# Moving casts, transfers and check steps in a hand-interleaved attention and FFN kernel

## The chip, the cores and the metric

The kernel runs on one core of one Trainium2 chip. The metric is device time in microseconds (us) of one execution of the whole program; lower is better. Its engines work side by side, each on its own list of instructions in order: TensorE (PE, matrix products), ScalarE (ACT), VectorE (DVE), GpSimd (POOL) and SyncE (SP, which here issues transfers). Instructions wait for each other through semaphores. Transfers (DMA) are issued by SP, ACT and POOL and run on 16 DMA engines.

## The reference

Causal attention with a decay bias, followed by a gated FFN:

```python
# q, k, v: (8 batches, 8 heads, 576, 64); s: (8, 8, 576)
scores = (q @ k^T) / sqrt(64)
cum    = cumsum(max(s, 0))
scores = where(causal, -1e9, scores + min(-(cum[i] - cum[j]), 0))
attn   = softmax(scores);  x = attn @ v          # as (4608 tokens, 512)
xn     = x / sqrt(mean(x^2) + 1e-6) * rms_g
g, val = xn @ w_gate, xn @ w_val                  # (512 -> 1536)
out    = (g * sigmoid(g) * val) @ w_out           # (1536 -> 512)
```

All inputs and outputs are float32; the products run in bf16.

## The kernel before, in words

The output's 4608 tokens are cut into 9 chunks of 512. `ffn(c)` computes one chunk: for each of 12 blocks `fb` of the hidden width, TensorE makes a gate product `Gp` (L668, four matmuls) and a value product `Vp` (L677), ScalarE a tanh `T` (L671), VectorE `U` = (T + 1) Gp (L680) and `Ht` = U Vp (L673); then four output blocks of 12 matmuls each (L690), copied out by ScalarE (`osb`, L695) and stored by a transfer on SP (L697). The products write `psF` buffers in PSUM, of which there are four in rotation: `Gp` is released by `U`, `Vp` by `Ht`.

Between these products the kernel calls `step()`, 36 times in a chunk. `slot` counts the calls, `phase()` the calls since the chunk began. Each call emits pieces of the attention of later batches, so TensorE's list is FFN products with attention pieces between them. The order is fixed when the program is built: lags are counted in steps, not in time. One call does, in this order:

- `x_scale` of the next block of x (L338, VectorE: x times its 1/rms `al_all` times `rms_g`), three steps after the second half of its attention output; then `xt_dma` (L348), a transpose on SP into `xnT`, which the FFN reads
- one item of `act_side` (ScalarE's casts, and issues of K and Q loads)
- if no block of x was moved: a transposing transfer of K or Q, `kq_dma` (L171, SP), from the list `x_seq`, at most every second step
- one item of `v_side` (issues of V loads, L175, on GpSimd's queue), in odd steps
- one item of `pool_side` (GpSimd's casts of K and Q to bf16, L141 and L149, or issues of loads of K, L155) and one of `dve_side` (VectorE's casts and magnitude checks, L369 and L375)
- a score step `S` (L250 matmuls, exps on ScalarE L274, causal mask on GpSimd L283), or else a transpose of x on TensorE, an attention output step `AV` (L300, L306, VectorE's L313 and L315, a sum of squares on ScalarE L321 or VectorE L325, 1/rms on GpSimd L328 and L331), and a transpose of K or Q on TensorE (`t_step`, L184)

A block is 128 rows of a batch's 576 (five blocks, the last of 64). For batches 0 and 1 K and Q are transposed on TensorE and copied by ScalarE (L192) or VectorE (L190); later ones use the transposing transfers. In batch 1 the cast of row group r of K or Q is one instruction of 128x512; "K2" below means K with r = 2. Before its first FFN chunk the kernel computes batch 0's attention without the stepper; the list of what follows, for batch 1, stands at L887 to L899. `need(c)` sees to it that the blocks of x that chunk c reads have been emitted.

`verdict()` (L741) reduces collected maxima to one flag, which says whether the fast path was exact enough; a general path follows it behind a branch. It needs VectorE reductions, a transpose of `stat` on TensorE (L750), another reduction, a second transpose (L754), an exp on ScalarE and five small VectorE instructions. It is emitted as one piece after chunk 7 (the eighth), before chunk 8, the last.

Of the kernel before, what the change touches and what calls it, by code (L numbers as in the profile page):

```python
# [12 lines left out]
AF = mybir.ActivationFunctionType  # L13
ALU = mybir.AluOpType
AX = mybir.AxisListType
# [4 lines left out]
DROP_MAX = 576.0 * 2.0 ** -24  # L20
RANGE_MAX = 75.0
# [5 lines left out]
def kernel(  # L27
# [91 lines left out]
    def psT32():  # L119
        return pp.tile([128, 512], FP32, name="psT32", tag="T", bufs=1)  # L120
# [14 lines left out]
    def cast(eng, b, w, r0, r1, h0=0, h1=H):  # L135
        o = kqn[:, b % 2, w, r0:r1, h0:h1, :]
        i = kq32[:, w].rearrange("p h (r d) -> p r h d", d=D)[:, r0:r1, h0:h1, :]
        if eng is nc.scalar:
            eng.activation(out=o, in_=i, func=AF.Copy)
        else:  # L140
            eng.tensor_copy(out=o, in_=i)  # L141
# [258 lines left out]
    def ready(lag, *key):  # L400
        return at(*key) + lag <= slot[0]
# [27 lines left out]
    def phase():  # L429

        return slot[0] - first[0]
# [167 lines left out]
    def step(bare=False):  # L599
# [13 lines left out]
                    done["XT", b, qb] = slot[0] + 4  # L613
                    moved = True
        run_side(act_side)
        if not moved and x_seq and slot[0] - last["X"] >= 2:
            b, w, c = x_seq[0]
            if (ready(2, "cast", b, 1) and ready(1, "S", b - 2, 4, 0)
                    and (w == 1 or ready(7, "K", b, c))):
                x_seq.pop(0)  # L620
                kq_dma(b, w, c)
                done["X", b, w, c] = last["X"] = slot[0]
                if b >= KB and (w, c) == (0, NSC - 1) and b + 2 < B:
                    casts(b + 2)
        bare = bare or chunk[0] == 0 and 30 <= phase() <= 33
        if slot[0] % 2 and not bare:
            run_side(v_side)
        if not bare:
            run_side(pool_side)
# [109 lines left out]
            lambda i=i: row(i) for i in range(3)] + [over])  # L739

    def verdict():  # L741
        nc.vector.tensor_reduce(out=stat[:, 0:1], in_=acc, axis=AX.X, op=ALU.max)
        okc = mp.tile([128, B * NSC], FP32, name="okc")
        nc.vector.tensor_scalar(out=okc, in0=ss_all, scalar1=SS_MAX, scalar2=None, op0=ALU.is_le)
        low = mp.tile([128, 1], FP32, name="low")
        nc.vector.tensor_reduce(out=low, in_=okc, axis=AX.X, op=ALU.min)
        nc.vector.tensor_scalar(out=stat[:, 3:4], in0=low, scalar1=-1.0, scalar2=1.0,
                                op0=ALU.mult, op1=ALU.add)
        ps = psT32()
        nc.tensor.matmul(ps[0:4, 0:128], lhsT=stat, rhs=ident_f, is_transpose=True)  # L750
        mx = mp.tile([4, 1], FP32, name="mx")
        nc.vector.tensor_reduce(out=mx, in_=ps[0:4, 0:128], axis=AX.X, op=ALU.max)
        ps2 = psT32()
        nc.tensor.matmul(ps2[0:1, 0:4], lhsT=mx, rhs=ident_f[0:4, 0:4], is_transpose=True)  # L754
        g = mp.tile([1, 8], FP32, name="g")
        nc.vector.tensor_copy(out=g[:, 0:4], in_=ps2[0:1, 0:4])

        nc.vector.tensor_scalar(out=g[:, 4:5], in0=g[:, 0:1], scalar1=g[:, 0:1], scalar2=8.0625,
                                op0=ALU.mult, op1=ALU.mult)
        nc.scalar.activation(out=g[:, 5:6], in_=g[:, 4:5], func=AF.Exp, scale=2.0)  # L760
        nc.vector.tensor_scalar(out=g[:, 5:6], in0=g[:, 5:6], scalar1=g[:, 2:3], scalar2=DROP_MAX,
                                op0=ALU.mult, op1=ALU.is_le)
        nc.vector.tensor_scalar(out=g[:, 6:7], in0=g[:, 4:5], scalar1=g[:, 1:2],
                                scalar2=RANGE_MAX, op0=ALU.add, op1=ALU.is_le)
        nc.vector.tensor_scalar(out=g[:, 7:8], in0=g[:, 3:4], scalar1=0.5, scalar2=None,
                                op0=ALU.is_le)
        nc.vector.tensor_tensor(out=g[:, 5:6], in0=g[:, 5:6], in1=g[:, 6:7], op=ALU.mult)
        nc.vector.tensor_tensor(out=flag_i, in0=g[:, 5:6], in1=g[:, 7:8], op=ALU.mult)


    with tc.manual_schedule():

# [114 lines left out]

        def done_cast(w):
            done["cast", 1, w] = slot[0]
        later(act_side, 1, [lambda r=r: cast(ACT, 1, 0, r, r + 1) for r in range(4)])  # L890
        later(pool_side, 1, [lambda: cast(POOL, 1, 0, 4, 5)])
        later(pool_side, 3, [lambda: done_cast(0)])
        later(pool_side, 4, [lambda: cast(POOL, 1, 1, 2, 3),
                             lambda: (cast(POOL, 1, 1, 3, 4), done_cast(1)),
                             lambda: cast(POOL, 1, 1, 4, 5)])
        later(dve_side, 3, [lambda r=r: cast(DVE, 1, 1, r, r + 1) for r in (0, 1)])
        later(v_side, 0, [
            lambda: load_v(1, 0), lambda: load_v(1, 1), lambda: load_v(1, 2),
# [202 lines left out]
```

## Time and profile before

| | us |
|---|---|
| time, median of 3 runs | 373.96 (373.92 to 374.02) |
| profiled execution, its own time | 374.31 |
| its span (first to last instruction) | 372.7 |
| TensorE busy | 349.3 |
| VectorE busy | 279.2 |
| ScalarE busy | 239.7 |
| GpSimd busy | 174.9 |

In the timeline view a row gives its start, its length, engine, source line, operation, output and inputs, and how many equal instructions were merged (x4); a bracket gives the idle time of the engine just before, and what ended it. PE rows that follow without a bracket run back to back, and their lengths overlap, since a matmul's end is counted at its result. The view of windows gives for a stretch of time each engine's busy time and count, in the order PE, PE's weight loads, DVE, ACT, POOL, then the granted TensorE clock and the DMA engines' share. SPq rows are transfers being issued on SP's queue, POOL rows of DMA_DIRECT2D transfers being issued by GpSimd.

### The profile page before, as it was taken

Reading aid. Unit: us, or ns where it says so; the run is one execution under the profiler, and the core shown is the slowest. Engines: PE = TensorE matmul, PEld = TensorE weight load, DVE = VectorE, ACT = ScalarE, POOL = GpSimd, SP = SyncE. Lnnn points to the kernel's source line nnn. Section 1 sums busy time; section 2 is a strip of 40 time slices with the busy share of each in tenths; the row PEclk is TensorE's granted clock in tenths of the full one; section 3 lists DMA queues with packets and bytes.
Section 4 is the critical chain, followed back from the end, with each engine's and each line's share of the span. In section 5 each row is a group of like instructions: output and inputs, shape, how many; then the busy total and the mean of one; then the engine's idle time right before and its main releaser. Section 6 shows DMA issues by size and latency. Waiting matters only on the chain. (4 is left out here: it accounts for less than half of the span.)

```text
span 372.7 us, 6935 instructions
## 1 busy us (share of the span) xinstructions
PE 349.3 (94%) x2356; PEld 162.5 (44%) x2356; DVE 279.2 (75%) x523; ACT 239.7 (64%) x626; POOL 174.9 (47%) x279
## 2 busy tenths in 40 slices
PE   1897999899999999899999999999999999999993
PEld 1553544353444444444444444444444444444441
DVE  6678988499887878788889898885488558837830
ACT  3977787457977597777768776776677644323321
POOL 5966724966757475779666734533322300000000
PEclk9999999999999999999999999999999999999999
DMA  7999999899958499949999997972300230020012
GB/s 234 175 235 246 161 222 186 139 219 214 189 114 111 44 208 155 167 57 205 152 181 203 135 117 158 103 64 44 104 18 14 44 106 3 0 84 31 0 48 73
DMA packets 125627, 46.22 MB, mean 124 GB/s; under 512 B 104913, under 2 KB 120785, under 8 KB 125585
## 3 DMA queue, kind: packets, MB, share of 16 engines
q0 software_dynamic: 59920, 11.80, 41.2%
q1 hardware_dynamic: 53040, 24.33, 33.6%
q10 hardware_dynamic: 12624, 9.59, 10.5%
q8 instruction: 20, 0.33, 0.4%
q14 instruction: 23, 0.18, 0.2%
HBM read 38.16 MB, written 9.44 MB: 128 GB/s over the span
## 5 line engine op out<-in xcount | busy, mean ns | idle before, releaser
L274 ACT ACTIVATE E<-psS,biasK 128x256 bf16<-128x256 f32 (+3 forms) x352 | 114.8, 415 | 19.7 <-PE psS L250 18.1
L668 PE MATMUL psF<-xnT,wg_sb 128*128 128x512 bf16 x432 | 111.1, 379 | 2.3 <-DMA xnT<-xs_sb 1.2
L677 PE MATMUL psF<-xnT,wv_sb 128*128 128x512 bf16 x432 | 111.1, 379 | 0.1
L690 PE MATMUL psF<-wout_sb,Ht 128*128 128x512 bf16 x432 | 102.3, 379 | 0.0
L283 POOL TENSOR_SCALAR_AFFINE_SELECT E<-E 128x512 bf16<-128x512 bf16 x72 | 52.3, 727 | 92.2 <-ACT E L274 91.6
L671 ACT ACTIVATE T<-psF 128x512 f32<-128x512 f32 x108 | 64.3, 597 | 42.0 <-PE psF L668 38.6
L680 DVE SCALAR_TENSOR_TENSOR U<-T,psF 128x512 bf16<-128x512 f32 x108 | 73.6, 681 | 22.2 <-ACT T L671 22.1
L673 DVE TENSOR_TENSOR Ht<-U,psF 128x512 bf16<-128x512 bf16 x99 | 67.6, 683 | 6.8
L668 PEld LDWEIGHTS <-wg_sb 128*128 128x128 bf16 x432 | 38.8, 98 | 46.7 <-issue 7.8
L677 PEld LDWEIGHTS <-wv_sb 128*128 128x128 bf16 x432 | 38.6, 98 | 42.8 <-issue 4.6
L690 PEld LDWEIGHTS <-Ht 128*128 128x128 bf16 x432 | 38.7, 98 | 42.1 <-issue 2.3
L338 DVE SCALAR_TENSOR_TENSOR xs_sb<-x_sb,al_all,g_row 128x512 bf16<-128x512 bf16 (+1 forms) x40 | 32.8, 822 | 16.1 <-POOL al_all L331 14.5
L695 ACT ACTIVATE osb<-psF 128x512 f32<-128x512 f32 x36 | 21.4, 595 | 33.7 <-PE psF L690 29.4
L321 ACT ACTIVATE xs_sb<-x_sb 128x512 bf16<-128x512 bf16 (+1 forms) x36 | 22.9, 639 | 22.1 <-DVE x_sb L315 22.0
L175 POOL DMA_DIRECT2D v_sb<-in_v_dram x40 | 34.9, 874 | 0.3 <-issue 0.3
L375 DVE TENSOR_TENSOR acc<-acc,mag 128x1280 bf16<-128x1280 bf16 x32 | 29.9, 950 | 0.4
L306 PEld LDWEIGHTS <-E 128*128 128x128 bf16 x320 | 23.1, 101 | 11.3 <-POOL E L283 0.8
L250 PE MATMUL psS<-kqT 64*128 64x256 bf16 (+2 forms) x304 | 26.8, 262 | 1.3 <-ACT E L274 1.1
L300 PEld LDWEIGHTS <-E 128*128 128x128 bf16 x256 | 21.2, 101 | 8.1 <-DVE x_sb L315 0.7
L328 POOL TENSOR_SCALAR al_all<-ss_all 128x1 f32<-128x1 f32 (+1 forms) x40 | 11.1, 277 | 28.2 <-ACT xs_sb L321 22.2
L331 POOL TENSOR_TENSOR al_all<-al_all,mhalf 128x1 f32<-128x1 f32 (+1 forms) x40 | 22.2, 556 | 3.3
L250 PEld LDWEIGHTS <-kqT 64*128 64x128 bf16 x320 | 10.3, 97 | 29.7 <-issue 28.7
(94 smaller groups left out, 282.1 us busy)
## 6 DMA issues: line engine op xcount, KB each, us to landing
out_dram<-osb SPq DMA_DIRECT2D x36, 256.0 KB, 2.3
kq<-in_q_dram ACTq DMA_DIRECT2D x6, 1024.0 KB, 8.2
v_sb<-in_v_dram POOLq DMA_DIRECT2D x32, 128.0 KB, 7.4
kq<-in_k_dram ACTq DMA_DIRECT2D x2, 1024.0 KB, 10.0
kqn<-in_k_dram POOLq DMA_DIRECT2D x16, 128.0 KB, 5.8
wg_sb<-in_moe_w_gate_dram POOLq DMA_DIRECT2D x2, 768.0 KB, 8.6
wv_sb<-in_moe_w_val_dram POOLq DMA_DIRECT2D x2, 768.0 KB, 11.7
wout_sb<-in_moe_w_out_dram POOLq DMA_DIRECT2D x1, 1536.0 KB, 14.4
```

The lines of the kernel that those rows point to most:

```text
L175: nc.gpsimd.dma_start(out=v_sb[0:n, b % 2, c, :, 0:64], in_=v[b, :, c * 128:c * 128 + n, :].rearrange("h p d -> p h d"))
L250: nc.tensor.matmul(pair[par][:, j * W:j * W + M], lhsT=kT, rhs=qT, start=(j == 0), stop=(j == nj - 1))
L274: nc.scalar.activation(out=eo, in_=ei, func=AF.Exp, scale=0.125, bias=biasK[:, kb, bh:bh + 1])
L283: nc.gpsimd.affine_select(out=Ev[:, :, 0:nq], in_=Ev[:, :, 0:nq], pattern=[[0, nh], [1, nq]], compare_op=ALU.is_ge, fill=0.0, base=0, chan ...
L338: nc.vector.scalar_tensor_tensor(out=xs_sb[0:n, (b * NSC + qb) % NX, :], in0=x_sb[0:n, (b * NSC + qb) % NX, :], scalar=al_all[0:n, col:col ...
L375: nc.vector.tensor_tensor(out=acc[:, sl], in0=acc[:, sl], in1=mag[:, sl], op=ALU.max)
L668: nc.tensor.matmul(Gp, lhsT=wg_sb[:, cc, fs], rhs=xnT[:, cc, x0:x0 + DM], start=(cc == 0), stop=(cc == CC - 1))
L671: nc.scalar.activation(out=T, in_=Gp, func=AF.Tanh, scale=0.5)
L673: nc.vector.tensor_tensor(out=Ht[:, fb - 1, :], in0=pend[0], in1=pend[1], op=ALU.mult)
L677: nc.tensor.matmul(Vp, lhsT=wv_sb[:, cc, fs], rhs=xnT[:, cc, x0:x0 + DM], start=(cc == 0), stop=(cc == CC - 1))
L680: nc.vector.scalar_tensor_tensor(out=U, in0=T, scalar=1.0, in1=Gp, op0=ALU.add, op1=ALU.mult)
L690: nc.tensor.matmul(Op, lhsT=Ht[:, fb, tb * 128:(tb + 1) * 128], rhs=wout_sb[:, fb, :], start=(fb == 0), stop=(fb == FB - 1))
```

## The change

Four edits, none of which changes what is computed.

1. Batch 1's casts: K2 and K3 go from ScalarE to GpSimd, right behind K4; Q2, Q3 and Q4 follow one item a step, in the same order as before. TensorE's steps stay where they are.
2. In `step`, a K or Q transfer is not emitted while the next block of x has its attention output emitted at least one step ago and is not yet scaled.
3. V loads are not emitted in chunk 0 from phase 34 on.
4. `verdict` is split: its first four VectorE instructions (`sums`) stay after chunk 7, the other three parts go into chunk 8 by way of `dve_side`, at phases 12, 15 and 18.

```diff
-        if not moved and x_seq and slot[0] - last["X"] >= 2:
+
+        if not moved and x_seq and slot[0] - last["X"] >= 2 and not (
+                scaled[0] < len(x_list) and ready(1, "AV", *x_list[scaled[0]], 1)):
...
-        if slot[0] % 2 and not bare:
+        if slot[0] % 2 and not bare and not (chunk[0] == 0 and phase() >= 34):
             run_side(v_side)
...
+        def sums():
+            nc.vector.tensor_reduce(out=stat[:, 0:1], in_=acc, axis=AX.X, op=ALU.max)
+            nc.vector.tensor_scalar(out=okc, in0=ss_all, scalar1=SS_MAX, scalar2=None, op0=ALU.is_le)
+            nc.vector.tensor_reduce(out=low, in_=okc, axis=AX.X, op=ALU.min)
+            nc.vector.tensor_scalar(out=stat[:, 3:4], in0=low, scalar1=-1.0, scalar2=1.0,
+                                    op0=ALU.mult, op1=ALU.add)
+        def turn():
+            ps = psT32()
+            nc.tensor.matmul(ps[0:4, 0:128], lhsT=stat, rhs=ident_f, is_transpose=True)
+            nc.vector.tensor_reduce(out=mx, in_=ps[0:4, 0:128], axis=AX.X, op=ALU.max)
+        def row():
+            ps2 = psT32()
+            nc.tensor.matmul(ps2[0:1, 0:4], lhsT=mx, rhs=ident_f[0:4, 0:4], is_transpose=True)
+            nc.vector.tensor_copy(out=g[:, 0:4], in_=ps2[0:1, 0:4])
+            nc.vector.tensor_scalar(out=g[:, 4:5], in0=g[:, 0:1], scalar1=g[:, 0:1], scalar2=8.0625,
+                                    op0=ALU.mult, op1=ALU.mult)
+        def flag():
+            nc.scalar.activation(out=g[:, 5:6], in_=g[:, 4:5], func=AF.Exp, scale=2.0)
+            nc.vector.tensor_scalar(out=g[:, 5:6], in0=g[:, 5:6], scalar1=g[:, 2:3], scalar2=DROP_MAX,
+                                    op0=ALU.mult, op1=ALU.is_le)
+            nc.vector.tensor_scalar(out=g[:, 6:7], in0=g[:, 4:5], scalar1=g[:, 1:2],
+                                    scalar2=RANGE_MAX, op0=ALU.add, op1=ALU.is_le)
+            nc.vector.tensor_scalar(out=g[:, 7:8], in0=g[:, 3:4], scalar1=0.5, scalar2=None,
+                                    op0=ALU.is_le)
+            nc.vector.tensor_tensor(out=g[:, 5:6], in0=g[:, 5:6], in1=g[:, 6:7], op=ALU.mult)
+            nc.vector.tensor_tensor(out=flag_i, in0=g[:, 5:6], in1=g[:, 7:8], op=ALU.mult)
+        return sums, turn, row, flag
...
-        later(act_side, 1, [lambda r=r: cast(ACT, 1, 0, r, r + 1) for r in range(4)])
-        later(pool_side, 1, [lambda: cast(POOL, 1, 0, 4, 5)])
-        later(pool_side, 3, [lambda: done_cast(0)])
-        later(pool_side, 4, [lambda: cast(POOL, 1, 1, 2, 3),
-                             lambda: (cast(POOL, 1, 1, 3, 4), done_cast(1)),
-                             lambda: cast(POOL, 1, 1, 4, 5)])
+        later(act_side, 1, [lambda r=r: cast(ACT, 1, 0, r, r + 1) for r in (0, 1)])
+        later(pool_side, 1, [
+            lambda: cast(POOL, 1, 0, 4, 5),
+            lambda: (cast(POOL, 1, 0, 2, 3), cast(POOL, 1, 0, 3, 4)),
+            lambda: (cast(POOL, 1, 1, 2, 3), done_cast(0)),
+            lambda: cast(POOL, 1, 1, 3, 4), lambda: done_cast(1), lambda: cast(POOL, 1, 1, 4, 5)])
...
+            if c == B:
+                dve_side.extend((lambda n=n: phase() >= n, f) for n, f in zip((12, 15, 18), steps))
             ffn(c)
             if c == B - 1:
-                verdict()
+                sums, *steps = verdict()
+                sums()
```

In the built program TensorE's list is the same before and after but for verdict's two transposes. ScalarE's differs by the two casts and the place of verdict's exp, VectorE's by the places of verdict's instructions. GpSimd's and SP's lists hold their casts, loads and transfers in a new order: the K and Q transfers come up to 18 steps later, and with them the loads of K for batches 6 and 7 (2 and 8 steps) and batch 7's casts of Q (2 steps).

More of the change, by code (lines that the diff above doesn't have):

```diff
@@ L741, in verdict @@
     def verdict():
-        nc.vector.tensor_reduce(out=stat[:, 0:1], in_=acc, axis=AX.X, op=ALU.max)
         okc = mp.tile([128, B * NSC], FP32, name="okc")
-        nc.vector.tensor_scalar(out=okc, in0=ss_all, scalar1=SS_MAX, scalar2=None, op0=ALU.is_le)
         low = mp.tile([128, 1], FP32, name="low")
-        nc.vector.tensor_reduce(out=low, in_=okc, axis=AX.X, op=ALU.min)
-        nc.vector.tensor_scalar(out=stat[:, 3:4], in0=low, scalar1=-1.0, scalar2=1.0,
-                                op0=ALU.mult, op1=ALU.add)
@@ L749, in verdict @@
-        ps = psT32()
-        nc.tensor.matmul(ps[0:4, 0:128], lhsT=stat, rhs=ident_f, is_transpose=True)
         mx = mp.tile([4, 1], FP32, name="mx")
-        nc.vector.tensor_reduce(out=mx, in_=ps[0:4, 0:128], axis=AX.X, op=ALU.max)
-        ps2 = psT32()
-        nc.tensor.matmul(ps2[0:1, 0:4], lhsT=mx, rhs=ident_f[0:4, 0:4], is_transpose=True)
         g = mp.tile([1, 8], FP32, name="g")
-        nc.vector.tensor_copy(out=g[:, 0:4], in_=ps2[0:1, 0:4])
-        nc.vector.tensor_scalar(out=g[:, 4:5], in0=g[:, 0:1], scalar1=g[:, 0:1], scalar2=8.0625,
-                                op0=ALU.mult, op1=ALU.mult)
@@ L760, in verdict @@
[L760 to L766, printed above, removed]
@@ L767, in verdict @@
-        nc.vector.tensor_tensor(out=g[:, 5:6], in0=g[:, 5:6], in1=g[:, 6:7], op=ALU.mult)
-        nc.vector.tensor_tensor(out=flag_i, in0=g[:, 5:6], in1=g[:, 7:8], op=ALU.mult)
+        def sums():
[4 more added lines that the diff above has]
+                                    op0=ALU.mult, op1=ALU.add)
```

## The prediction

> **What bounds the kernel now.** I read the page's busy times first, then TensorE's own timeline for every place where it stood idle, then the view of what ended each of these waits on the engine that was late. Numbers are us unless marked.
>
> ```profile
> PE 349.3 (94%) x2356; PEld 162.5 (44%) x2356; DVE 279.2 (75%) x523; ACT 239.7 (64%) x626; POOL 174.9 (47%) x279
> ```
>
> TensorE is the bound: 94% busy, the granted clock full in every slice. Only its idle places can be won. The start (up to 30.7) and the last transfer are not touched. Of the rest, these are the ones that the change can reach, and one large one (72.75) that it leaves:
>
> ```profile
> 36.83 0.23 PE L184 MATMUL psT<-ident_bf,kqn 128*128 128x128 bf16 x1 [1.14 <-ACT kqn L139]
> ...
> 39.66 0.23 PE L184 MATMUL psT<-ident_bf,kqn 128*128 128x128 bf16 x1 [0.48 <-POOL kqn L141]
> ...
> 72.75 0.40 PE L357 MATMUL psT<-ident_bf,xs_sb 128*128 128x128 bf16 x4 [1.49 <-DVE xs_sb L338]
> ...
> 154.05 1.02 PE L668 MATMUL psF<-xnT,wg_sb 128*128 128x512 bf16 x4 [1.16 <-DMA xnT<-xs_sb]
> ...
> 334.56 0.27 PE L750 MATMUL psT<-ident_f,stat 128*4 128x128 f32 x1
> 335.20 0.16 PE L754 MATMUL psT<-ident_f,mx 4*1 4x4 f32 x1 [0.37 <-DVE mx L752]
> 335.42 1.02 PE L668 MATMUL psF<-xnT,wg_sb 128*128 128x512 bf16 x4
> ```
>
> The bracket is the idle time before a row and what ended it. TensorE's program is the same before and after, instruction by instruction, but for the two transposes of verdict. So the forecast is a matter of which waits shrink and which grow.
>
> **Part 1: casts of batch 1.** ScalarE loses two casts of K (r = 2 and 3; the row of two of its casts at 32.27 is 1.14, so 0.6 each); GpSimd gains them, and its order becomes K4, K2, K3, V issue, Q2, mask, Q3, V issue, Q4. The pause that takes them:
>
> ```profile
> 32.04 0.89 POOL L175 DMA_DIRECT2D v_sb<-in_v_dram  x1
> 36.33 0.66 POOL L283 TENSOR_SCALAR_AFFINE_SELECT E<-E 128x512 bf16<-128x512 bf16 x1 [3.40 <-ACT E L274]
> ```
>
> From 32.1: K2 and K3 at 0.63 (the cast at 31.49) end near 33.4, the V issue of 0.89 at 34.3. Q2 has to wait for q, which lands when VectorE's first Q cast starts, 34.86, so it ends near 35.5. The mask waits for ScalarE's exps, which end 0.5 earlier without the cast between them (35.7), so it runs to 36.4, and Q3 to 37.0 (at 0.63) or 37.6 (at 1.18, the cast at 36.95). TensorE wants K2 and K3 at 35.4: they are there, 1.14 goes. It then wants Q3 1.3 earlier than its present 38.9, at 37.7: there too, 0.48 goes. Up to 1.6 is on offer. ScalarE's lost 1.2 frees nothing else, it waits for TensorE around it.
>
> What is late next is VectorE:
>
> ```profile
> 34.90:48.50 13.60, 11.98 (x103) 6.44 (x102) 13.25 (x24) 10.34 (x26) 8.34 (x11) 1.00 1.35 175
> ...
> 38.97 1.32 DVE L375 TENSOR_TENSOR acc<-acc,mag 128x1280 bf16<-128x1280 bf16 x1
> ...
> 42.17 0.81 DVE L375 TENSOR_TENSOR acc<-acc,mag 128x1280 bf16<-128x1280 bf16 x1
> ...
> 44.77 0.67 DVE L673 TENSOR_TENSOR Ht<-U,psF 128x512 bf16<-128x512 bf16 x1
> ...
> 46.07 0.38 PE L668 MATMUL psF<-xnT,wg_sb 128*128 128x512 bf16 x1
> ```
>
> From 34.9, set by the landing of q, to 48.5 it is busy 13.25 of 13.60, in work whose order the change leaves alone, so it can't come forward. TensorE's gate product of fb = 6 (46.07) writes the psF buffer that Ht of fb = 4 releases, at 45.44; with 0.06 from release to start (the row at 72.75 starts 0.06 after its releaser's end at 72.69) TensorE can be at most 0.57 ahead there. The other buffers on the way allow more (V of fb = 5: 44.98 against 43.58; V of fb = 6: 47.81 against 46.65). After 48.5 VectorE's gaps are waits for ScalarE and TensorE, so the lead is kept, and the chain through GpSimd to 72.75 starts with VectorE at 63.55 and moves with it: that wait stays 1.49. Contention shifts the 0.57: L375 takes 1.32 beside GpSimd's casts and 0.81 alone, and the casts move off it by half (gain some 0.25) and onto VectorE's two Q casts of 0.43 (loss of the same size). Bounds: 1.6 gained, or 0.2 lost (0.57 less two contended instructions at 0.4 to 0.5). I take 0.55, nearest to the buffer's row.
>
> The Trainium skill, "SBUF - State Buffer", section "Who interferes with whom", says that a VectorE instruction with two SBUF inputs and a GpSimd instruction that reads SBUF do not share: the second to start blocks until the first is done. The trace has 1.32 against 0.81, less than a whole cast of 0.63; by the rule in full the chain would lose 0.63 for each cast met, and this part's result would be the second rival's.
>
> **Part 2: no K or Q transfer ahead of a block of x.** A K or Q transpose is now held from one step after the block's AV until its transpose is issued. The wait at 154.05, read on SyncE's queue and VectorE:
>
> ```profile
> 148.26 0.75 DVE L338 SCALAR_TENSOR_TENSOR xs_sb<-x_sb,al_all,g_row 128x512 bf16<-128x512 bf16 x1 [0.72 <-POOL al_all L331]
> ...
> 148.86 1.19 SPq L171 DMA_TRANSPOSE kqT<-kqn  x1
> 150.15 1.20 SPq L348 DMA_TRANSPOSE xnT<-xs_sb  x1
> ```
>
> The block is scaled at 149.01, but SyncE issues a Q transpose from 148.86 to 150.05, and the block follows at 150.15 and lands 3.9 later, 154.0, just behind the Q transpose (4.8 from 148.86, 153.6). Afterwards that transpose stands behind the block; the block issues at 149.07 and, at 2.4 to 3.9 as the xnT transposes here take, lands at 151.5 to 153.0. TensorE's product would start 0.2 after its last score product's 152.62, at 152.8. The wait becomes 0 to 0.2: gain 1.0 to 1.2, floor 0 if the landing is set by the K loads that share the engines. I take 1.15, from the issue times.
>
> The price is that K and Q transposes come later, by up to 18 steps of about 1.03. Every score step keeps its place, with at least 11 steps from the last transpose that it needs (12 before). The tightest in time that I find: batch 5, second key block, at 195.57, needs two that now issue behind the x block at 176.95, so at 178.3 and 179.6; with that region's 9.7 they land at 189.3, 4.5 before TensorE with its new lead of 1.7. K loads of batches 6 and 7 follow later for the same reason, 2 to 8 steps, with dozens of steps to their use. Cost 0. One wait of 0.3 near 210.5, behind GpSimd's cast at 207.27, may go as that cast moves two steps; not counted.
>
> **Part 3: no V issue in the last steps of chunk 0.** The issue at 73.11 (0.95) moves two casts back on GpSimd. The wait at 72.75 ends before it, the V block is wanted 25 steps later. 0, from 0.3 lost to 0.3 gained by contention.
>
> **Part 4: verdict.** Before, TensorE goes from 334.56 to 335.42 on it, 0.86. After, the transposes stand among the products of the last chunk, three steps (2.6) apart, so nothing waits; they still cost TensorE about 0.27 and at most 0.16 by their rows, less their overlap: 0.35. VectorE gets 0.28, 0.35 and some 0.7 in three places where it idles 0.25 per pair of products; Ht ends 2.3 after its V product starts and is wanted 3.46 after, so a delay of 0.8 is covered. ScalarE's exp of 0.20 has 1.13 of idle beside it. Gain 0.5 (0.35 to 0.6).
>
> **Sum.** The profiled execution took 374.31 (span 372.7, 1.6 around it), 0.35 above the median of 373.96. 374.31 - 0.55 - 1.15 - 0.5 = 372.1; less 0.35 as that execution stood, 371.75, said as 371.7.
>
> **The rivals.**
> - VectorE doesn't hold TensorE, because its chain shortens too: all of 1.6 arrives, 370.7. For it: L375 has 0.5 to give back. Against: 13.25 of 13.60. Chance 0.12.
> - GpSimd's casts block VectorE: two full casts of 0.63 less 0.5 returned delay Ht by 0.75, part 1 turns from 0.55 into -0.2: 372.5. For it: 1.32 against 0.81. Chance 0.15.
> - The order on SyncE does not do what it says: the landing at 154.0 is the engines' (K loads from 148.18 in flight), part 2 gives 0.1: 372.8. Against: the 1.08 between scaling and issue is the queue's. Chance 0.10.
> - Slower: late Q transposes. Held ones issue in bunches behind the x blocks of batches 4 and 5, where landings already take 7 to 11.7. From 14.2 on the step at 195.57 waits, and from 16.4 on that one wait has eaten the 2.2; at 17.5 it ends at 374.9 with its successor waiting too. The longest landing of such a transpose is 11.7. Chance 0.07.
>
> **How the numbers follow.** My case has 0.56; its own range is 371.2 to 372.3. The predicted time is its 371.7. A change of 0.2% (0.75) is about what can be told from none, so faster means under 373.2: my case, the first rival, 0.12 of the second and 0.04 of the third, which other shifts can carry over that line: 0.84; same, what is left of these two: 0.09; slower 0.07. The range from 370.4 to 373.2 takes in the first three rivals and leaves out the fourth.
>
> **What would show it.** After: no idle of 1.14 and 0.48 near 36 to 40, but short waits of TensorE for VectorE's Ht or U between 38 and 47; the wait near 72 as long as before; no Q transpose between scaling and xnT near 149, and no DMA wait at the start of the fourth chunk; verdict's two rows without idle. It is wrong if L250 rows wait for DMA kqT, if VectorE's Ht near 45 ends later than 45.4, or if the wait at the second chunk's end grows.

## The result, and the profile after

The changed kernel takes 373.13 us (median of 20 runs, 371.37 to 373.95); the kernel before, run beside it, 374.14 (20 runs, 373.64 to 379.08). The ratio is 0.9959, 95% interval 0.9941 to 0.9977: 1.5 us faster, where 2.2 was predicted. (The two medians alone are 1.0 apart; the means of the 20 runs give the 1.5.) The ratios here and below leave out runs over 1.5% above the fastest of their kernel: one of b3_fused at 373.9, and one of 379.71 of the kernel before beside m1 to m4. The profiled execution took 373.4 with a span of 371.5, against 374.31 and 372.7.

The page of the changed kernel, engine totals:

```profile
PE 346.3 (93%) x2312; PEld 162.7 (44%) x2356; DVE 277.1 (75%) x523; ACT 238.7 (64%) x624; POOL 176.4 (47%) x281
```

TensorE's busy time looks 3.0 smaller, but its count does too: 2312 matmul records against 2356, with the same 2356 weight loads. 44 records are missing from this trace, so this line can't be compared with the one before; positions can. (A busy share that falls together with its count says nothing of the work.) ScalarE's two casts fewer and GpSimd's two more are the whole visible change here.

TensorE's timeline of the changed kernel, the rows that answer those of the prediction (start, length, engine, line, operation, output and inputs, idle before and what ended it). The line numbers have moved by two or more: L668 is now L670, L750 is L758, L754 is L763.

```profile
37.83 1.02 PE L670 MATMUL psF<-xnT,wg_sb 128*128 128x512 bf16 x4 [0.88 <-DVE Ht L675]
...
72.33 0.40 PE L357 MATMUL psT<-ident_bf,xs_sb 128*128 128x128 bf16 x4 [1.52 <-DVE xs_sb L338]
...
152.96 1.02 PE L670 MATMUL psF<-xnT,wg_sb 128*128 128x512 bf16 x4 [0.45 <-issue]
...
156.50 0.40 PE L250 MATMUL psS<-kqT 64*128 64x256 bf16 x4 [0.55 <-ACT E L274]
...
343.75 0.27 PE L758 MATMUL psT<-ident_f,stat 128*4 128x128 f32 x1
346.54 0.16 PE L763 MATMUL psT<-ident_f,mx 4*1 4x4 f32 x1
```

The two waits for casts (1.14 and 0.48) are gone, and a wait of 0.88 for Ht stands in their place. The wait near 72 is as it was. The wait for xnT fell from 1.16 to 0.45 ("issue" here is the landing: the transpose landed at 152.87, 0.09 ahead of the product), and a new one of 0.55 follows it at 156.50. The two transposes of verdict stand among products and nothing waits for them.

One hold more shows no bracket, since the lengths of PE rows overlap. It is the one that the prediction named: Ht of fb = 4 on VectorE and the gate product of fb = 6 behind it.

```profile
44.90 0.67 DVE L675 TENSOR_TENSOR Ht<-U,psF 128x512 bf16<-128x512 bf16 x1
...
45.62 1.02 PE L670 MATMUL psF<-xnT,wg_sb 128*128 128x512 bf16 x4
```

Ht ends at 45.57 and the product starts 0.05 later; before, it started 0.62 later.

Because TensorE's list is the same in all these kernels but for verdict's two rows, its lead can be read instruction by instruction. This table takes the start of the same weight load in each execution, counted from the first gate product of chunk 0, less that of before (negative is ahead); the columns are places by the time of before. Later sections use it too.

| lead over before at | 48.5 | 80 | 140 | 160 | 200 | 230 | 350 |
|---|---|---|---|---|---|---|---|
| changed kernel | -0.57 | -0.53 | -0.50 | -0.59 | -1.13 | -1.28 | -1.83 |
| part 1 alone (p1_casts) | -0.30 | -0.29 | -0.28 | -0.33 | -0.82 | -0.82 | -0.82 |
| part 2 alone (p2_hold) | +0.01 | +0.03 | +0.06 | -0.04 | -0.59 | -0.76 | -0.76 |
| part 3 alone (p3_vhold) | +0.43 | +0.44 | +2.10 | +2.08 | +2.09 | +2.09 | +2.09 |
| part 4 alone (p4_verdict) | -0.05 | -0.04 | -0.03 | -0.13 | -0.12 | -0.12 | -0.67 |
| m1_qlate | -1.96 | -1.96 | -1.93 | -2.04 | -2.60 | -2.77 | -3.31 |
| m2_nochecks | -1.75 | -1.72 | -1.67 | -0.88 | -1.38 | -1.54 | -2.09 |
| m3_vearly | -0.29 | -1.90 | -1.89 | -2.00 | -2.56 | -2.73 | -3.27 |
| m4_khold | -0.88 | -0.85 | -0.14 | -0.23 | +0.50 | +0.20 | +0.36 |
| b1_best | -1.18 | -2.81 | -2.80 | -2.90 | -2.97 | -3.14 | -3.68 |
| b3_fused | -1.96 | -3.58 | -4.10 | -4.88 | -5.19 | -5.35 | -5.90 |
| b4_nopart2 | -1.18 | -2.80 | -2.80 | -2.59 | -2.02 | -1.11 | -1.65 |
| p1_qlate | -1.70 | -1.67 | -1.64 | -1.73 | -2.17 | -2.16 | -2.17 |

So the changed kernel wins 0.5 at the casts, 0.1 at the block of x, 0.5 at a place between 180 and 200 that the prediction counted nothing for, 0.15 near 210, and 0.55 at the verdict: 1.83. The span shrinks by 1.2 only. The last store is issued at 365.65 in place of 367.36, 1.71 sooner, but the span ends 5.85 after it, and before 5.34.

The chain of work that ended last, of the changed kernel, around the new wait (start, length, what):

```profile
149.92 0.75 DVE mag L369
150.67 0.02 issue
150.69 2.02 DVE acc L375 x2
152.71 0.10 DVE rZ L313
152.81 0.02 issue
152.83 0.44 DVE x_sb L315
153.27 0.02 issue
153.29 0.05 ACT xs_sb L321
...
153.83 0.19 ACT xs_sb L321
154.02 0.48 ACT osb L697
154.50 0.73 ACT E L274 x2
155.23 0.50 ACT T L673
```

This is the story of the give-back: VectorE is busy with magnitude checks (L369, L375) up to 152.7, so x_sb comes at 153.26; ScalarE's sum of squares (L321) waits for it, and the output copy, the tanh and the exps of the score step stand in line behind. The next score product needs those exps.

### The profile page after: what moved, and what is told of

Same layout as the page of the kernel before. It is cut to its first block, busy times and chain, and to the rows that moved or that the text cites. A ratio compares the mean times of both kernels' runs of the same rounds, so it can differ in the third digit from the quotient of the medians.

```text
span 371.5 us, 6891 instructions
## 1 busy us (share of the span) xinstructions
PE 346.3 (93%) x2312; PEld 162.7 (44%) x2356; DVE 277.1 (75%) x523; ACT 238.7 (64%) x624; POOL 176.4 (47%) x281
## 4 chain that ended last, share of the span: by engine, by line
PE 61%; DVE 14%; POOL 8%; issue 6%; DMA 5%; ACT 4%; ACTq 0%; POOLq 0%; DVEq 0%
PE psF L692 19%; PE psF L670 17%; PE psF L679 17%; PE psS L250 3%; DVE U L682 3%; DMA kq<-in_q_dram 3%; DVE Ht L675 2%; DVE x_sb L315 2%; POOL v_sb L175 2%; DVE xs_sb L338 2%; ACT E L274 2%; DVE acc L375 2%; POOL E L283 2%; DMA kq<-in_k_dram 1%; POOL kqn L141 1%
## 5 line engine op out<-in xcount | busy, mean ns | idle before, releaser
L670 PE MATMUL psF<-xnT,wg_sb 128*128 128x512 bf16 x426 | 110.3, 379 | 2.6 <-DVE Ht L675 0.9
L679 PE MATMUL psF<-xnT,wv_sb 128*128 128x512 bf16 x408 | 109.3, 380 | 1.4
L692 PE MATMUL psF<-wout_sb,Ht 128*128 128x512 bf16 x419 | 100.5, 379 | 0.5 <-issue 0.2
L283 POOL TENSOR_SCALAR_AFFINE_SELECT E<-E 128x512 bf16<-128x512 bf16 x72 | 51.5, 716 | 85.5 <-ACT E L274 85.1
L670 PEld LDWEIGHTS <-wg_sb 128*128 128x128 bf16 x432 | 38.8, 98 | 47.1 <-issue 8.0
L338 DVE SCALAR_TENSOR_TENSOR xs_sb<-x_sb,al_all,g_row 128x512 bf16<-128x512 bf16 (+1 forms) x40 | 31.9, 800 | 16.4 <-POOL al_all L331 14.8
L321 ACT ACTIVATE xs_sb<-x_sb 128x512 bf16<-128x512 bf16 (+1 forms) x36 | 23.0, 641 | 22.3 <-DVE x_sb L315 22.0
L375 DVE TENSOR_TENSOR acc<-acc,mag 128x1280 bf16<-128x1280 bf16 x32 | 29.0, 922 | 0.4
L250 PE MATMUL psS<-kqT 64*128 64x256 bf16 (+2 forms) x304 | 26.8, 262 | 1.7 <-ACT E L274 1.1
L141 POOL CAST kqn<-kq 128x512 bf16<-128x512 f32 (+1 forms) x30 | 20.7, 710 | 5.8 <-DMA kq<-in_k_dram 3.7
```

The costliest lines, as they stand in the source:

```text
L250: nc.tensor.matmul(pair[par][:, j * W:j * W + M], lhsT=kT, rhs=qT, start=(j == 0), stop=(j == nj - 1))
L283: nc.gpsimd.affine_select(out=Ev[:, :, 0:nq], in_=Ev[:, :, 0:nq], pattern=[[0, nh], [1, nq]], compare_op=ALU.is_ge, fill=0.0, base=0, chan ...
L338: nc.vector.scalar_tensor_tensor(out=xs_sb[0:n, (b * NSC + qb) % NX, :], in0=x_sb[0:n, (b * NSC + qb) % NX, :], scalar=al_all[0:n, col:col ...
L375: nc.vector.tensor_tensor(out=acc[:, sl], in0=acc[:, sl], in1=mag[:, sl], op=ALU.max)
L670: nc.tensor.matmul(Gp, lhsT=wg_sb[:, cc, fs], rhs=xnT[:, cc, x0:x0 + DM], start=(cc == 0), stop=(cc == CC - 1))
L679: nc.tensor.matmul(Vp, lhsT=wv_sb[:, cc, fs], rhs=xnT[:, cc, x0:x0 + DM], start=(cc == 0), stop=(cc == CC - 1))
```

## Experiments: the four parts, one at a time

All comparisons are of runs on one chip, part by part beside the kernel before. The runs of one program spread over 2 to 4 us there, so the ratios are known to about 0.15 to 0.3%, and the table above decides where they can't.

**Part 1 alone.** The edit is the last hunk of the diff but one, the casts.

> Part 1 alone, in the kernel before: K2 and K3 cast by GpSimd, Q2 to Q4 one item a step. My theory (VectorE, whose chain starts with q's landing, holds TensorE at the gate products): the two waits of 1.14 and 0.48 near 37 and 40 go, about 1.0 of the 1.6 comes back as waits for Ht, TensorE is 0.4 to 0.6 ahead from 46 on and keeps it to the end: time 0.9985 to 0.999 of before. First rival (all arrives): 1.6 ahead at 46, 0.9957. Second rival (GpSimd's casts block VectorE for their full 0.63): 0.2 behind at 46, 1.0005. Within this kernel q's landing is the thing to read: if it comes 0.5 later than before, as in the whole change, the wait sits at the gate product of fb = 3, on Ht of fb = 1; if it comes at the old time, at fb = 6 on Ht of fb = 4, as the prediction had it.

Measured: 0.9991 of before (0.9975 to 1.0006). TensorE is 0.30 ahead after the casts, under the 0.4 to 0.6 expected, and 0.82 ahead after 192. TensorE's timeline of this kernel, and VectorE's and GpSimd's ahead of it:

```profile
37.24 1.02 PE L668 MATMUL psF<-xnT,wg_sb 128*128 128x512 bf16 x4 [0.50 <-DVE Ht L673]
39.17 1.02 PE L677 MATMUL psF<-xnT,wv_sb 128*128 128x512 bf16 x4 [0.68 <-DVE U L680]
```

```profile
30.20 3.56 DVE L375 TENSOR_TENSOR acc<-acc,mag 128x1280 bf16<-128x1280 bf16 x2
...
31.34 1.73 POOL L141 CAST kqn<-kq 128x512 bf16<-128x512 f32 x3
```

Again VectorE holds TensorE: the longest waits are at fb = 3, as in the whole change, and the gate product of fb = 6 again starts 0.05 behind Ht of fb = 4 (45.62 and 45.57). But VectorE is late for another cause. Here q was there in time, and the second of two checks (L375) was held for the length of GpSimd's three casts: 3.56 for the pair, where 1.56 is the pair undisturbed. All of this is ahead of 34.9, where the prediction began to count.

**Part 2 alone.** The edit is the first hunk.

> Part 2 alone: no transpose of K or Q ahead of a block of x. The prediction's step: 1.0 to 1.2 ahead from 154 to the end, 0.997 of before. What the trace of the whole change suggests: the wait of 1.16 near 154 falls to about 0.4, and about 0.6 of what is won is given back near 156.5 to a score product that waits for ScalarE's exps, so about 0.1 is left at 160 (0.9997), with some more from 192 on if the 0.5 that the whole change wins there belongs to this part. Third rival (the engines set the landing, not the queue): the wait near 154 stays above 1.0. Fourth rival: L250 rows that wait for kqT, slower than before.

Measured: 0.9984 (0.9964 to 1.0004). Its two rows on TensorE:

```profile
153.35 1.02 PE L670 MATMUL psF<-xnT,wg_sb 128*128 128x512 bf16 x4 [0.23 <-issue]
157.11 0.40 PE L250 MATMUL psS<-kqT 64*128 64x256 bf16 x4 [0.77 <-ACT E L274]
```

The wait for xnT falls from 1.16 to 0.23, so the order on SyncE does what it says, and 0.77 of it comes back 3.8 later. At 160 the lead is 0.04: part 2 by itself wins nothing at the place that it was made for. It wins 0.5 at 192 and 0.17 near 210. The third rival falls (the wait did not stay), and no row of L250 waits for kqT.

**Part 3 alone.** The edit is the second hunk.

> Part 3 alone: no V issue on GpSimd in the last steps of chunk 0. Prediction: 0, the wait of 1.49 near 72.7 stays within 0.2 and TensorE's position after 80 is within 0.3 of before; 1.000 of before. Against it: if V issues on GpSimd set the chain to that wait through the casts behind them, the wait shrinks and the kernel gains up to 1.5 (0.996); if the held V block comes late, a wait for v_sb appears and the kernel is slower.

Measured: 1.0002 (0.9983 to 1.0022). The wait near 72 stays, no wait for v_sb appears. The profiled execution lost 1.7 at one place, a wait for xnT at the start of the third chunk (116.18, 1.48 idle), with the same transfers in the same order as before; the median landing of the xnT transposes in this execution was 3.9 against 3.4. What made the transfers slower in that one execution is not known. It shows how much a single execution can differ.

**Part 4 alone.** The edit is the splitting of verdict.

> Part 4 alone: the verdict's steps spread over the last chunk. Prediction: 0.5 (0.35 to 0.6) between 334 and 350, nothing anywhere else: 0.9987 of before. If the small VectorE instructions delayed the products of the last chunk, U or Ht waits would show between 340 and 355 and the gain would be under 0.3. It is also the measure of what a kernel with the same work up to 334 varies by: any shift ahead of 334 in this kernel is not the change.

Measured: 0.9993 (0.998 to 1.0006), and by the table 0.55 between 334 and 350. The lead ahead of 334, where nothing is changed, is 0.03 to 0.13; in part 3 alone it is 0.43 the other way at 48.5, ahead of its edit. Positions vary by that much from execution to execution there, and by 1.7 once, so a step in the table counts where several executions share it.

## Experiments: what each part runs into

These four start from the changed kernel with one small edit each. What else an edit moves is said with it.

**Q casts of VectorE one step later.**

```diff
-        later(dve_side, 3, [lambda r=r: cast(DVE, 1, 1, r, r + 1) for r in (0, 1)])
+        later(dve_side, 4, [lambda r=r: cast(DVE, 1, 1, r, r + 1) for r in (0, 1)])
```

> The changed kernel with VectorE's two casts of Q one step later, behind Ht of fb = 1 and fb = 2; nothing else is moved. Theory: after the change the gate product of fb = 3 (37.83) waits 0.88 because Ht of fb = 1 stands on VectorE behind the Q casts, which wait for q's landing. With the casts behind it, Ht of fb = 1 is ready some 0.7 to 1.0 sooner, that wait falls to under 0.3, and TensorE is 0.3 to 0.6 further ahead by 46 unless a later Ht takes it back (VectorE has the same work to do by 48.5): 0.9984 to 1.000 of the changed kernel. Rival (GpSimd's casts hold VectorE back, q's landing does not matter): the wait stays 0.5 to 0.9. A cost to look for: the first transpose of Q on TensorE waits for VectorE's cast.

Measured: 371.69 (371.08 to 371.95), 0.9907 of before (0.9882 to 0.9933). The wait of 0.88 is gone, and no other has come: the lead at 48.5 is 1.96, far over the 0.9 to 1.2 that was expected. (It is over the offer of 1.6 too: by the positions of the weight loads the two waits of before are 1.31 and 0.65, since a bracket counts from the modelled end of the row before.) VectorE in this kernel:

```profile
34.26 0.69 DVE L682 SCALAR_TENSOR_TENSOR U<-T,psF 128x512 bf16<-128x512 f32 x1 [0.25 <-ACT T L673]
35.01 0.43 DVE L141 CAST kqn<-kq 128x512 bf16<-128x512 f32 x1
35.35 0.68 DVE L675 TENSOR_TENSOR Ht<-U,psF 128x512 bf16<-128x512 bf16 x1
...
43.17 0.67 DVE L675 TENSOR_TENSOR Ht<-U,psF 128x512 bf16<-128x512 bf16 x1
43.77 0.81 DVE L375 TENSOR_TENSOR acc<-acc,mag 128x1280 bf16<-128x1280 bf16 x1
```

In the changed kernel VectorE stood idle for 1.39 up to 35.39 for q, with U and Ht of fb = 1 behind the casts; here U fills that gap. The edit moves more than the casts: `dve_side` gives out one item a step, so the checks in line behind the casts move a step back too, and the second L375 (43.77) now stands behind Ht of fb = 4 (43.17), where it stood ahead of it (42.29 against 44.90 in the changed kernel). That takes another 0.8 out of what TensorE waits for. This run does not tell the two apart. The stretch from 34.9 to 48.5, which the prediction showed as VectorE's 13.25 of 13.60, reads like this now (PE, PE's weight loads, DVE, ACT, POOL, clock, DMA):

```profile
34.90:48.50 13.60, 13.60 (x114) 7.16 (x113) 13.25 (x26) 10.88 (x27) 9.99 (x12) 1.00 1.44 197
```

VectorE is as busy as it was, 13.25, though with 26 instructions for 24, and TensorE has no idle left. A full VectorE held TensorE only through what stood in its list ahead of a needed U or Ht: the late landing and the checks.

**The magnitude checks left out near 150.** This kernel doesn't compute the checks of K of batch 3 and of K and Q of batch 4.

```diff
-            lambda w=w: check_mag(b, w), lambda: check_max(0), lambda: check_max(1),
+            () if (b, w) in ((3, 0), (4, 0), (4, 1)) else
+            (lambda w=w: check_mag(b, w), lambda: check_max(0), lambda: check_max(1))) + (
```

> The changed kernel without the magnitude checks (VectorE's L369 and L375) of K of batch 3 and of K and Q of batch 4: that part of the computation is left out. Theory: the wait of 0.55 near 156.5, with which the change gives back what it won near 153, is ScalarE's exps standing behind a sum of squares that waits for x_sb, which stands on VectorE behind these checks (150.7 to 152.7). Without them the wait near 156.5 falls under 0.15 and 0.4 to 0.6 is won there. Rival (ScalarE's own exps take that long, two score steps follow each other too closely): the wait stays 0.4 or more, and only other places change.

Measured: 373.41 (372.24 to 376.33), 0.9969 (0.9944 to 0.9994). The wait near 156.5 is gone, with the 0.62 of lead that the changed kernel loses there. TensorE came to this place 0.33 later than in the changed kernel, so this run alone shows about half of it as the checks'; b3_fused below shows the rest. It came later because the wait for xnT ahead of it grew:

```profile
153.03 1.02 PE L671 MATMUL psF<-xnT,wg_sb 128*128 128x512 bf16 x4 [1.96 <-issue]
```

Without the checks' marks the K loads come sooner, five of them are issued between 141.4 and 150.6, and the transpose of x took 6.13 to land in place of 4.21. A second thing is to be seen in its row of the table, first column: 1.75 ahead at 48.5, with VectorE's casts of Q where the change has them. The first Q cast could start at 34.38 in this execution, 1.0 sooner than in the profiled one of the changed kernel, and so most of part 1's offer arrived.

**V loads of batch 2 sooner, and the hold from phase 24.**

```diff
-            (early if b else later)(v_side, 6 if b else 16, [
+            (early if b else later)(v_side, 6 if b else 8, [
...
-        if slot[0] % 2 and not bare and not (chunk[0] == 0 and phase() >= 34):
+        if slot[0] % 2 and not bare and not (chunk[0] == 0 and phase() >= 24):
```

> The changed kernel with the V loads of batch 2 issued 8 steps sooner, and the hold of part 3 in chunk 0 from phase 24 on in place of 34, so that two V issues of 0.95 on GpSimd leave the steps ahead of the second chunk. Theory: GpSimd's own list (V issues and casts ahead of al_all) is the chain to the wait of 1.5 near 72.3, which part 3 moved a V issue away from too late to matter: the wait falls by 0.9 to 1.5, 0.996 to 0.9975 of the changed kernel. Rival (the wait is VectorE's and ScalarE's order, or a landing): the wait stays within 0.3 of 1.5.

Measured: 371.86 (371.09 to 375.01), 0.9938 (0.9905 to 0.997). The wait of 1.5 near 72 is gone altogether; TensorE's row in this kernel has no bracket:

```profile
70.87 0.40 PE L357 MATMUL psT<-ident_bf,xs_sb 128*128 128x128 bf16 x4
```

So the wait that the prediction left as it was came from GpSimd's own queue: two V issues of 0.95 (66.22 and 69.24 in the changed kernel) ahead of al_all. Part 3 moved the V issue behind it. In this execution the check near 31 was held again (3.55 for the pair) and part 1 brought 0.29 only, as in p1_casts.

**K loads held too.**

```diff
-            pool_side.extend((lambda: free(0) and slot[0] % 2 == 0, lambda c=c: key(c)) for c in range(NSC))
+            pool_side.extend((lambda: free(0) and slot[0] % 2 == 0 and not (
+                scaled[0] < len(x_list) and ready(1, "AV", *x_list[scaled[0]], 1)),
+                lambda c=c: key(c)) for c in range(NSC))
```

> The changed kernel with the loads of K (issued by GpSimd) also held while a block of x waits to be scaled, as the change does for the transposes on SyncE. Theory: the landing of 4.2 after issue near 149 is lengthened by K loads in flight; without them it is 2.4 to 3.2, and the wait of 0.45 near 153 goes (the score product near 156.5 then waits longer by as much, so the time stays within 0.3). Rival (the landing is the transpose's own or that of Q transposes ahead of it): the wait of 0.45 stays.

Measured: 375.76 (373.96 to 376.38), 1.0017 (0.9996 to 1.0038). The mechanism is as expected: with no K load ahead of it (one is issued 1.2 behind it, at 150.27) the transpose of x landed 2.30 after its issue, not 4.21, and TensorE had no idle at that product. The score product behind it then waited 1.05. But the held loads make the K transposes late, as a row that no other kernel here has:

```profile
189.74 0.40 PE L250 MATMUL psS<-kqT 64*128 64x256 bf16 x4 [1.21 <-DMA kqT<-kqn]
```

The transpose that it needs landed at 189.61; in the changed kernel the same one landed at 180.21, for a product at 187.87. That is the fourth rival's mechanism, and the slack of 7.7 that the change left against it there. Another 0.7 had gone before: at 128.68 a gate product waits 0.67 for U, behind an L338 on VectorE of 2.00, 0.88 in the changed kernel.

## Experiments: both moves together, and what is left

**Both moves** (the edits of m1_qlate and m3_vearly).

> The changed kernel with both moves that won alone: VectorE's casts of Q one step later, and the V loads of batch 2 sooner with the hold from phase 24. If they are independent (about 1.0 to 1.4 of each), TensorE is 2.2 to 2.8 ahead of the changed kernel by 80 and the time is 0.987 to 0.990 of before. Where it can be lost again: the landing of xnT near 150 (if it follows TensorE's lead, the wait stays under 0.3; if transfers set it, it grows to 1 or more) and the exps near 155, whose wait grew from 0.55 to 0.8 with a lead of 1.2 and would be 0.8 to 1.0.

Measured: 370.45 (369.51 to 371.54), 0.9875 (0.9852 to 0.9898). The lead over the changed kernel at 80 is 2.28. The wait for xnT near 151 is 0.36, the one for exps 0.63.

**The checks out of the steps that emit an attention output.** On top of both moves, with all computed:

```diff
-        run_side(dve_side)
+        if chunk[0] < 1 or phase() < 25 or can_s() or not can_av():
+            run_side(dve_side)
...
-            lambda w=w: check_mag(b, w), lambda: check_max(0), lambda: check_max(1),
-            lambda w=w: done.__setitem__(("check", b, w), slot[0])))
+            lambda w=w: check_mag(b, w), lambda: check_max(0),
+            lambda w=w: (check_max(1), done.__setitem__(("check", b, w), slot[0]))))
```

> The kernel of both moves, with VectorE's magnitude checks not emitted, from phase 25 of a chunk on, in a step that emits an attention output product and no score step (and the last part of a check and its mark in one item); all is computed, and the lists of TensorE, ScalarE and SyncE stay as they are. Theory (the exps near 155 are late because x_sb stands behind a check on VectorE): the wait of a score product there falls from some 0.8 to under 0.2, and half a microsecond to 0.8 is won against the kernel of both moves (0.998). Rival (the place is ScalarE's own): the wait stays, 1.000.

Measured: 369.02 (368.24 to 373.9), 0.9843 (0.9818 to 0.9868): 5.9 us under before, the best kernel of this study. ScalarE's timeline around the block of x, first of the changed kernel, then of this one:

```profile
153.29 0.63 ACT L321 ACTIVATE xs_sb<-x_sb 128x512 bf16<-128x512 bf16 x1 [2.00 <-DVE x_sb L315]
```

```profile
148.61 0.63 ACT L321 ACTIVATE xs_sb<-x_sb 128x512 bf16<-128x512 bf16 x1 [0.75 <-DVE x_sb L315]
```

```profile
149.46 1.02 PE L671 MATMUL psF<-xnT,wg_sb 128*128 128x512 bf16 x4 [0.38 <-issue]
...
152.38 0.39 PE L250 MATMUL psS<-kqT 64*128 64x256 bf16 x4
```

ScalarE waits 0.75 for x_sb, not 2.00, and the score product (152.38) has no bracket: between 140 and 160 TensorE wins 0.78, where both moves alone win 0.10. Another 0.5 comes near 90. The rest of its distance to b1_best (0.8 at 48.5) is the check near 31, which was held in that execution (3.55) and not in this one (1.56).

**Both moves without part 2.** The condition of the first hunk is taken out of b1_best.

> The kernel of both moves with part 2 undone: transposes of K and Q may be issued ahead of a block of x again. By the trace of part 2 alone (0.2 won at 157, 0.56 at 192 that part 1 alone wins as well), part 2 is worth 0.1 to 0.4 here: 1.0003 to 1.001 of the kernel of both moves, with a wait for xnT of about 1.2 near 151 and none near 155. By the prediction's price (1.15, nothing given back) it is worth 1.0 to 1.2: 1.003.

Measured: 371.25 (370.37 to 373.15), 0.9897 (0.9877 to 0.9916). At 160 part 2 is worth 0.31 here, as the first case expected has it; the kernel then loses 1.5 more up to 230, with waits for exps of 0.45 and 0.46 near 193 and 197 and one of 1.05 for Ht at 209.40. By the medians part 2 is worth 0.8 here (the two intervals overlap), nearer the prediction's 1.15 than my expectation, but later and through other rows than the one that it aimed at. One profile each does not show whether those later waits come from the missing part 2.

**Part 1 with the Q casts later, in the kernel before.**

> Part 1 alone in the kernel before, with VectorE's casts of Q one step later. If what kept 1.0 of part 1's 1.6 back is VectorE's place for the Q casts (behind q's landing and ahead of Ht of fb = 1), TensorE is 1.3 to 1.6 ahead at 46, where part 1 alone was 0.55 ahead: 0.996 to 0.9975 of before, and the wait near 72.7 stays 1.5. If it is the amount of VectorE's work up to 48.5, as the prediction had it, the lead at 46 stays at 0.5 to 0.7 and a wait for Ht shows at fb = 5 or 6. If GpSimd's casts hold the check L375 near 31 back by 2 us as in the run of part 1 alone, part of it is lost in either case.

Measured: 373.04 (372.61 to 375.24), 0.9964 (0.9942 to 0.9986). The lead at 48.5 is 1.70, against 0.30 of part 1 alone, and the wait near 71 is 1.52. In this execution the first Q cast waited for q up to 35.41, as late as in the changed kernel, and most of the offer arrived all the same; 0.26 of the 1.96 was held back again by VectorE, at fb = 6. And at 154, with no part 2 in it, TensorE found xnT landed and then waited 0.94 for the exps:

```profile
151.45 1.02 PE L668 MATMUL psF<-xnT,wg_sb 128*128 128x512 bf16 x4
...
155.38 0.39 PE L250 MATMUL psS<-kqT 64*128 64x256 bf16 x4 [0.94 <-ACT E L274]
```

From 140 to 160 the lead grows by no more than 0.11 in any kernel that has the checks in their old place, whether or not part 2 is in it and whatever it waits for xnT (ten of them lie between 0.02 and 0.11, b4_nopart2 loses 0.21, by its wait for xnT). In the ten, the score product behind the block is what sets the time there.

## Why the prediction was right, and where it was not

**The total** was right in sign and within its range (370.4 to 373.2; measured 373.13), at the slow end of it. That it stayed inside is in part luck: part 2 brought 1.06 less than its price, and some 0.65 that was not counted (0.5 between 180 and 200, 0.15 near 210) made up for part of it.

**Part 1** was right in its mechanism: VectorE's list, which has no bracket from q's landing to Ht of fb = 4, holds the gate product of fb = 6. In the five kernels that have part 1 and the Q casts in the change's place, that product starts 0.05 behind that Ht, and the end of Ht gives the lead. Times here count from the first gate product of chunk 0, and 0.57 is the room that the prediction read:

| | end of Ht of fb = 4, less before | 0.57 less that | lead at 48.5 |
|---|---|---|---|
| changed kernel | 0.00 | 0.57 | 0.57 |
| part 1 alone (p1_casts) | +0.27 | 0.30 | 0.30 |
| m3_vearly | +0.28 | 0.29 | 0.29 |
| m4_khold | -0.31 | 0.88 | 0.88 |
| m2_nochecks | -1.18 | 1.75 | 1.75 |

The wait of 0.88 for Ht of fb = 1, at fb = 3, was not foreseen. It is the longest to be seen, but it did not set the lead: no row of VectorE from the first Q cast (35.39) to the end of that Ht (45.57) is idle for TensorE, so Ht of fb = 4 would have ended where it did without it. (The prediction's sign of being wrong, an Ht that ends later than 45.4, is met by the span's clock alone: the first gate product of this execution starts 0.11 later than before.)

The step that failed is "in work whose order the change leaves alone, so it can't come forward". With the same order, the end of that Ht moved by 1.46 from execution to execution. The first cast that waited for q started between 34.04 and 35.41; the second check near 31 took 0.8 or 2.8 beside the three casts; the second Q cast took from 0.42 to 0.91. So part 1 was worth 0.3 to 0.9 where a late q or a held check stood ahead (the first four rows), and 1.75 where neither did: the first rival's case and mine are the same order of work in different executions. That the changed kernel's profiled execution has 0.57, next to 0.55, is luck in the size. Its Ht of fb = 4 ended just where it ended before, because a first Q cast 0.42 later and a second 0.43 longer were made up for by checks 0.63 shorter and 0.22 less of idle.

With the Q casts and the checks one step later, the product of fb = 6 starts 0.38 behind that Ht in m1_qlate and 0.31 in b3_fused, so the hold is gone; in p1_qlate, b1_best and b4_nopart2 it is 0.05 again, with leads of 1.2 to 1.7.

**The second rival**, casts that block VectorE, was put too low in one way: the row of 1.32 against 0.81 was read as less than a whole cast. L375 began at 38.97 and GpSimd's cast ran from 38.98 to 39.60; 39.60 and 0.69 make 40.29, the end of L375. It had waited for the whole cast. The same 0.69 stands between the end of the last cast and the end of L375 in the pair of 2.46 in the kernel before (32.12 and 32.81) and in p1_casts (33.07 and 33.76). The rule of the Trainium skill that the prediction named ("SBUF — State Buffer", section "Who interferes with whom", that the other fully blocks) agrees with these three rows. The other half of that rule, that the one that starts second is the one that waits, does not: in these rows L375 starts 0.01 to 0.40 ahead of the cast, and waits. What kept the price low in p1_casts is that the blocking fell before 34.9, where VectorE otherwise waits for q.

**Part 2** failed in its price. The wait did shrink, to 0.45 and 0.23 (predicted 0 to 0.2), the order on SyncE did what was said, and K and Q later cost nothing in the changed kernel. The step that failed is "the wait becomes 0 to 0.2: gain 1.0 to 1.2": I did not ask what is late next, as I had for part 1. The profile before had it, on ScalarE and TensorE:

```profile
155.96 0.86 ACT L274 ACTIVATE E<-psS,biasK 128x256 bf16<-128x256 f32 x2
```

```profile
156.98 0.39 PE L250 MATMUL psS<-kqT 64*128 64x256 bf16 x4
```

The two exps end at 156.8 and the score product follows 0.16 later without idle; less the 0.06 from release to start, only some 0.1 of the 1.16 was to be won there. The runs gave 0.09 in the changed kernel and 0.10 in p2_hold.

**What made up for it** was not counted: 0.5 between 180 and 200. VectorE's scaling of x (L338) and three casts of GpSimd meet, and change which of them waits. VectorE and GpSimd, kernel before and changed kernel:

```profile
182.13 1.24 DVE L338 SCALAR_TENSOR_TENSOR xs_sb<-x_sb,al_all,g_row 128x512 bf16<-128x512 bf16 x1
...
181.11 1.71 POOL L149 CAST kqn<-kq 128x512 bf16<-128x512 f32 x3
```

```profile
181.60 0.74 DVE L338 SCALAR_TENSOR_TENSOR xs_sb<-x_sb,al_all,g_row 128x512 bf16<-128x512 bf16 x1
...
180.57 2.24 POOL L149 CAST kqn<-kq 128x512 bf16<-128x512 f32 x3
```

One of the two is 0.5 longer, and it is GpSimd in the kernels where the wait of 0.57 at 192 is gone (the changed kernel, p1_casts, p2_hold, m1_qlate, m3_vearly, p1_qlate), VectorE where it stays (before, p3_vhold, p4_verdict, b1_best). In all ten L338 starts 0.08 to 0.09 ahead of the third cast, so the records do not tell the two outcomes apart. None of the three without parts 1 and 2 has the good one, but b1_best, with both parts and a longer lead, has the bad one too. Whether this 0.5 is the change's or a draw of the execution is open, and that the turn of these rows is what removes the wait was seen only as going together. The wait near 210, named as uncounted, gave 0.15.

**Part 3** was right: nothing. **Part 4** was right: 0.55 for 0.5.

**The fourth rival** did not come (no wait for kqT); it took a further hold of K loads to make it real. The first rival's gain in part 1 came once by itself (m2_nochecks, with an early q); with the further edit of m1_qlate it was 1.2 to 1.96 in five executions.

## What to carry to other kernels

When a wait is taken away, look up the instruction that comes just behind it on the same engine and how long before it its own inputs were ready; if that is 0.1, the gain is 0.1, whatever the wait was. An engine that is busy 97% of a stretch can hold another one and still be relieved without doing less: ask which late or unhurried things (here casts that wait for a landing, and checks) stand in its list ahead of something urgent, and move them one place back. And where a step rests on a landing or on two engines meeting, one profile gives one draw of it: look at several executions before pricing it.

## What was not expected of the hardware

Two VectorE checks (L375) and GpSimd's casts near 31 met in three ways. VectorE's rows in the kernel before and in part 3 alone (that of part 1 alone stands above):

```profile
30.35 2.46 DVE L375 TENSOR_TENSOR acc<-acc,mag 128x1280 bf16<-128x1280 bf16 x2
```

```profile
30.33 1.56 DVE L375 TENSOR_TENSOR acc<-acc,mag 128x1280 bf16<-128x1280 bf16 x2
```

The kernel before and part 3 alone have the same instructions there, and in both the cast starts 0.40 after the second check (31.49 and 31.09, 31.47 and 31.07). In one the check waits for the cast, 0.9 longer; in the other the cast takes 0.89 in place of 0.63 and the check nothing. With three casts in a row (p1_casts) the check waited for all three, 2.0, though it had started 0.40 ahead of the first by the records. In the six executions with three casts in a row and this distance of 0.40, the check waited for all three in four (p1_casts, m3_vearly, b1_best, b4_nopart2) and for none in two (m1_qlate, m2_nochecks). The records do not show what decides it. A change that puts more casts in a row there raises the price of a lost draw from 0.9 to 2.0.

The landing of one transpose of x near 149, 128x512, was 2.30 with no K load ahead of it and one issued 1.2 behind it (m4_khold), 3.2 to 4.6 with the usual two or three around it, and 6.13 with five issued in the 9 us around it (m2_nochecks). That is one landing in each kernel.
